# Weight tiles of 512 columns read with a column step of four, w_out four rows per descriptor, the band from 256-column products, and a new order of the first steps, in a fused convolution and SwiGLU kernel

## Chip, cores and metric

The kernel runs on one core of a Trainium2 chip. The metric is device time in microseconds (us) of one execution. Lower is better. Verdicts use a threshold of 2%. The differences in this case are far below it, near 0.1%, so most of the study is about which parts of a small change arrive in the time, and which do not.

## The reference

A causal convolution over the sequence (7 taps for each of 8 heads, the taps being a softmax of a small weight table), then a SwiGLU block. Shapes: x is 8 x 4096 x 192, so 32768 tokens of width 192; d_ff is 1536. All is float32 outside; the kernel computes in float16 with float32 accumulation.

```python
out  = einsum('hk,bskhg->bshg', softmax(weight), windows(x_pad))   # 7 taps, 8 heads
g    = out @ w_gate            # 192 -> 1536
val  = out @ w_val
y    = (g * sigmoid(g) * val) @ w_out                              # 1536 -> 192
```

## The kernel before

Tokens go through in 64 blocks of 512. A block has 12 *steps*; step n computes 128 of the 1536 hidden columns by three pairs of matmuls (gate on the upper 64 rows of the array, val on the lower 64, at once), a silu on ScalarE and a product on VectorE. *Slots* of down matmuls (times w_out) are put between the steps. The convolution of later blocks is a set of small matmuls with a band matrix, hidden among the steps.

The start is special. Nothing can run before the band is made from the 8 x 7 taps. The first four blocks' inputs (tiles xe) are convolved by `early(e)`, turned by matmuls in `eturn(e)`, and only then can gate steps run. All loads that cast from float32 to float16 are issued by GpSimd, in this order: input of block 0, first and second piece of the weights, input of block 1, third piece, w_out, more input.

```python
    def load_w(f0, f1):                       # gate and val columns f0 to f1, three DMAs
        for half, src, i0, i1, s0 in (...):
            nc.gpsimd.dma_start(out=w16[Q*half : Q*half+Q, i0:i1, f0:f1], in_=src[..., f0:f1]...)
    def load_wo(c0, c1):                      # 128 rows of w_out per chunk, 768 B each (f32)
        nc.gpsimd.dma_start(out=wo16[:, c0:c1, :], in_=moe_w_out[...].rearrange("(c p) d -> p c d", p=P))
    ...
    xe_load(0)
    load_w(0, 384)
    load_w(384, 1024)
    xe_load(1)
    load_w(1024, Dff)
    load_wo(0, 6)
    load_wo(6, NCH)
    # ... cut: more input loads, preparations of the band
    keep_warm(7)              # filler matmuls of 512 columns
    spread_taps()             # 16 tiny matmuls, then two spreads on VectorE
    keep_warm(2)
    make_wide()               # four products of 512 columns, copied out by ScalarE and VectorE
    early(0, ...)
    eturn(0, ...)
    # gate_val(n):
            nc.tensor.matmul(o, w16[p0 : p0 + Q, k, ts(j, P)], xc[b][k][p0 : p0 + Q, 0:TB], ...)
    # main loop, first block: early(1) after step 4, eturn(1) after step 6, slot 1 after step 7,
    # slot 2 (with early(2) inside) after step 10, eturn(2) after step 17;
    # a slot at step n waits for the silu of step n - 2 ("row halves swap banks")
```

## Time and profile before

| | before |
|---|---|
| median time | 793.78 us (792.71 to 794.28, 4 runs) |
| span of the profiled execution | 792.0 us |
| TensorE busy | 784.0 us |
| first gate matmul | 9.97 us |
| step 23 begins (all start effects are over) | 37.59 us |
| from step 36 to the end | 739.99 us |

The page's busy table and the chain of work that ended last (shares of the span, by engine):

```profile
PE 784.0 (99%) x12018; PEld 493.9 (62%) x12018; DVE 584.1 (74%) x933; ACT 522.2 (66%) x910; POOL 67.4 (9%) x93
...
PE 97%; DMA 1%; POOL 1%; DVE 0%; ACT 0%; issue 0%; POOLq 0%
```

TensorE is the limit nearly everywhere. Its costliest groups (line, engine, operation, output and inputs, partitions x elements, count; then busy us, mean ns of one, idle time before them):

```profile
L545 PE MATMUL val<-xc,w 64*128 64x512 f16 x2304 | 539.1, 376 | 0.2 <-DVE tm L486 0.2
L545 PE MATMUL gate<-xc,w 64*128 64x512 f16 x2304 | 539.2, 376 | 0.0
L545 PEld LDWEIGHTS <-w 64*128 64x128 f16 x4608 | 221.0, 94 | 212.7 <-issue 1.2
```

The matmuls of a pair overlap each other and the next pair: a duration of 376 ns does not mean that one takes 376 ns of TensorE. What counts is the spacing of the pairs, 0.215 us. The PEld line is the load of the weights into the array, 94 ns each, beside the matmuls.

The start on TensorE (timeline: start us, duration us, then as above, with idle time and what ended it in brackets):

```profile
5.43 1.58 PE L326 MATMUL taps<-spread,shift 128*128 128x512 f16 x4
7.57 0.83 PE L380 MATMUL cv<-xe,wide 64*64 64x72 f16 x64 [0.56 <-ACT wide L338]
8.89 1.14 PE L438 MATMUL turn<-ident,tme 128*128 128x128 f16 x15 [0.50 <-ACT tme L398]
9.97 0.39 PE L545 MATMUL gate<-xc,w 64*128 64x512 f16 x1
...
13.72 0.22 PE L380 MATMUL cv<-xe,wide 64*64 64x72 f16 x1
14.50 0.72 PE L380 MATMUL cv<-xe,wide 64*64 64x48 f16 x63 [0.56 <-DMA xe<-in_x_dram]
15.15 0.39 PE L545 MATMUL gate<-xc,w 64*128 64x512 f16 x1
...
30.45 0.72 PE L438 MATMUL turn<-ident,tme 128*128 128x128 f16 x10 [0.34 <-DVE o_sb L627]
```

early(0) waits for the band at 7.57 us; early(1) waits for the input of block 1, which lands at 14.46 us; and the second turn waits for the output copies of block 0 at 30.45 us.

### The profile page before, as it was taken

The page shows a single profiled execution, that of the slowest core. Times are in us where ns is not written, and L with a number is a line of the kernel's source. Part 1 is how long each engine was busy: PE and PEld are TensorE (multiplying, and loading weights), DVE is VectorE, ACT ScalarE, POOL GpSimd, SP SyncE. Part 2 cuts the span into 40 slices and gives each one's busy share as a digit, 9 for nine tenths or more (in the row PEclk, how much of TensorE's full clock was granted, in tenths as well). Part 3 has the DMA queues.
Part 4 walks back from the last instruction along what each step waited for, and adds up shares of the span by engine and source line. Part 5 has one row for each costly group of instructions (what it writes and reads, how often), then busy time and mean ns, then how long its engine had stood idle before and what let it go on. Part 6 is the DMA issues. An engine that isn't in the chain of part 4 may idle for free.

```text
span 792.0 us, 28590 instructions
## 1 busy us (share of the span) xinstructions
PE 784.0 (99%) x12018; PEld 493.9 (62%) x12018; DVE 584.1 (74%) x933; ACT 522.2 (66%) x910; POOL 67.4 (9%) x93
## 2 busy tenths in 40 slices
PE   8999999999999999999999999999999999999997
PEld 4666666666666666666666666666666666666665
DVE  7677777777777867767777777777777777777775
ACT  5676766666666666757666666666667667676664
POOL 8111010010100101001010000100001010000000
PEclk9999999999999999999999999999999999999999
DMA  9999577786857778567894769858587794726311
GB/s 131 149 204 146 125 116 118 164 124 146 105 120 152 129 147 119 120 126 125 155 140 113 117 112 165 128 133 118 112 154 121 150 115 118 136 81 116 80 42 42
DMA packets 214961, 99.23 MB, mean 125 GB/s; under 512 B 148776, under 2 KB 213936, under 8 KB 213936
## 3 DMA queue, kind: packets, MB, share of 16 engines
q1 hardware_dynamic: 167424, 78.75, 49.3%
q0 software_dynamic: 47136, 18.45, 21.7%
q8 instruction: 94, 1.54, 0.8%
q14 instruction: 35, 0.29, 0.1%
q10 hardware_dynamic: 272, 0.20, 0.1%
HBM read 36.90 MB, written 41.16 MB: 99 GB/s over the span
## 4 chain that ended last, share of the span: by engine, by line
PE 97%; DMA 1%; POOL 1%; DVE 0%; ACT 0%; issue 0%; POOLq 0%
PE gate L545 61%; PE acc L571 32%; PE cv L469 2%; PE val L545 1%; DMA xe<-in_x_dram 1%; POOL w L162 0%; POOL xe L97 0%; PE acc L592 0%; PE cv L380 0%; PE turn L438 0%; DVE h L556 0%; ACT sig L554 0%; DVE o_sb L627 0%; DVE tm L486 0%; ACT o_sb L731 0%
## 5 line engine op out<-in xcount | busy, mean ns | idle before, releaser
L556 DVE TENSOR_TENSOR h<-sig,val 128x512 f16<-128x512 f16 x768 | 507.7, 687 | 195.4 <-PE val L545 192.9
L554 ACT ACTIVATE sig<-gate 128x512 f16<-128x512 f32 x768 | 458.5, 597 | 234.9 <-PE val L545 207.4
L545 PE MATMUL val<-xc,w 64*128 64x512 f16 x2304 | 539.1, 376 | 0.2 <-DVE tm L486 0.2
L545 PE MATMUL gate<-xc,w 64*128 64x512 f16 x2304 | 539.2, 376 | 0.0
L545 PEld LDWEIGHTS <-w 64*128 64x128 f16 x4608 | 221.0, 94 | 212.7 <-issue 1.2
L571 PEld LDWEIGHTS <-h 64*128 64x128 f16 x6096 | 257.8, 94 | 66.0 <-issue 6.1
L571 PE MATMUL acc<-wo,h 64*128 64x192 f16 x6096 | 298.8, 243 | 0.0
L97 POOL DMA_DIRECT2D x<-in_x_dram x40 | 31.6, 792 | 437.0 <-ACT sig L554 429.9
L486 ACT CAST tm<-cv 128x480 f16<-128x480 f32 x60 | 30.6, 562 | 22.1 <-PE cv L469 22.1
L486 DVE CAST tm<-cv 128x480 f16<-128x480 f32 x60 | 36.6, 652 | 2.6
L627 DVE COPY o_sb<-acc 128x384 f32<-128x384 f32 x63 | 34.7, 550 | 0.0
L497 POOL COPY tm<-tm 128x1280 f16<-128x1280 f16 x15 | 18.8, 1252 | 137.3 <-DVE tm L486 129.1
L626 ACT COPY o_sb<-acc 128x384 f32<-128x384 f32 x63 | 30.1, 478 | 0.0
L469 PE MATMUL cv<-x,band 64*32 64x240 f16 x960 | 18.2, 265 | 0.0
L469 PEld LDWEIGHTS <-band 64*32 64x32 f16 x960 | 10.1, 91 | 4.9 <-issue 4.7
L132 POOL MEMSET x<- 6x192 f16 x7 | 1.7, 248 | 59.7 <-PE cv L469 59.6
L97 POOL DMA_DIRECT2D xe<-in_x_dram x9 | 6.0, 692 | 0.4 <-issue 0.3
L643 PE MATMUL warm<-fill 128*128 128x512 f16 x9 | 4.2, 628 | 1.2 <-DVE fill L91 1.2
L398 ACT CAST tme<-cv 128x288 f16<-128x288 f32 x8 | 2.9, 401 | 2.5 <-PE cv L380 2.5
L380 PE MATMUL cv<-xe,wide 64*64 64x48 f16 (+1 forms) x256 | 3.2, 192 | 1.1 <-ACT wide L338 0.6
L380 PEld LDWEIGHTS <-wide 64*64 64x64 f16 x256 | 2.7, 108 | 2.5 <-ACT wide L338 1.1
L438 PE MATMUL turn<-ident,tme 128*128 128x128 f16 x45 | 3.3, 220 | 0.8 <-ACT tme L398 0.5
(53 smaller groups left out, 40.0 us busy)
## 6 DMA issues: line engine op xcount, KB each, us to landing
out_dram<-o_sb SPq DMA_DIRECT2D x63, 384.0 KB
scr<-tm SPq DMA_DIRECT2D x105, 130.0 KB
x<-x SPq DMA_DIRECT2D x28, 480.0 KB
x<-in_x_dram POOLq DMA_DIRECT2D x24, 480.0 KB, 9.4
x<-in_x_dram POOLq DMA_DIRECT2D x7, 468.0 KB, 7.4
xc<-scr SPq DMA_TRANSPOSE x180
scr<-tm SPq DMA_DIRECT2D x15, 104.0 KB
wo<-in_moe_w_out_dram POOLq DMA_DIRECT2D x2, 288.0 KB, 6.3
```

Of the source, the lines that this page charges most:

```text
L97: nc.gpsimd.dma_start(out=t[p0 + i0 : p0 + i1, w0 - at : w1 - at, :], in_=bass.AP(tensor=x_flat.tensor, offset=(t0 + size * w0 - pad + i0) ...
L380: nc.tensor.matmul(o[Q * c : Q * c + Q, at : at + w], wide[Q * r : Q * r + Q, a, h, :], xe[e][Q * r : Q * r + Q, c : 2 * G : 2, h * grp : ...
L469: nc.tensor.matmul(banks[r][32 * c : 32 * c + 32, t * w : t * w + w], band[Q * r : Q * r + Q, h, :], x16[u][Q * r : Q * r + Q, NG * c : NG ...
L486: eng(tm[u][:, NG * r : NG * r + NG, 2 * grp * hp : 2 * grp * hp + 2 * grp].rearrange("p g (t e) -> p g t e", t=2), banks[r][:, 0 : 2 * w] ...
L497: seq(nc.gpsimd.tensor_copy(tm[u][:, :, SL * Q : 4 * Q], tm[u][:, :, 0:Q]))
L545: nc.tensor.matmul(o, w16[p0 : p0 + Q, k, ts(j, P)], xc[b][k][p0 : p0 + Q, 0:TB], start=(k == 0), stop=(k == SL - 1),)
L554: silu[n] = seq(nc.scalar.activation(sg, g, AF.Silu)).ins
L556: seq(nc.vector.tensor_tensor(hj, sg, v, op=ALU.mult))
L571: nc.tensor.matmul(acc[b][bank][:, s, :], hj[p0 : p0 + Q, ts(2 * bank + s, P)], wo16[p0 : p0 + Q, j, :], start=(not second and j == 0 and ...
L626: seq(nc.scalar.copy(o_sb[:, 0:2, :], acc[b][0]))
L627: seq(nc.vector.tensor_copy(o_sb[:, 2:4, :], acc[b][1]))
L643: nc.tensor.matmul(warm, fill[:, 0:P], fill, start=True, stop=True, skip_group_check=True,)
```

## The change

Its intent: make the band with less work; load equal pieces of 512 weight columns; load w_out in fewer, longer rows (four rows of w_out, 3072 B, are contiguous when hidden column 4p + e sits on partition p). The price of that is that the gate weights must be read with a column step of four. The first 22 steps get a new order. The diff, cut to its core:

```diff
-    w16 = wpool.tile([P, SL, Dff], fp16, tag="w16", name="w16")
+    WF = Dff // 3; E = WF // P                       # 512 columns, step 4
+    w16 = [wpool.tile([P, SL, WF], fp16, tag=f"w16{m}", name="w16") for m in range(3)]
@@ load_wo
-                out=wo16[:, c0:c1, :],
-                in_=moe_w_out[P * c0 : P * c1, :].rearrange("(c p) d -> p c d", p=P),
+                out=wo16[:, E * m : E * m + E, :].rearrange("p e d -> p (e d)"),
+                in_=moe_w_out[WF * m : WF * m + WF, :].rearrange("(p e) d -> p (e d)", p=P),
@@ the first input window: 56 rows, issued second; its tile cleared over 64 rows
-                windows(xe[e], 0, 0, EO, 0, 1, i0=pad)
                 windows(xe[e], 0, 0, EO, 1, w1)
+                windows(xe[e], 0, 0, EO, 0, 1, i0=pad, i1=Q - 2)
@@ loads
-    load_w(0, 384); load_w(384, 1024); xe_load(1); load_w(1024, Dff); load_wo(0, 6); load_wo(6, NCH)
+    load_w(0); load_w(1); xe_load(1); load_w(2); load_wo(0); load_wo(1); load_wo(2)
@@ band: 2 tap matmuls instead of 16, one spread of 256 columns instead of two of 512,
@@ four products of 256 columns instead of four of 512      [cut]
-    keep_warm(2)
+    keep_warm(5, P)                                  # fillers of 128 columns
@@ gate_val
-                        w16[p0 : p0 + Q, k, ts(j, P)],
+                        w16[m][p0 : p0 + Q, k, e::E],
@@ order of the first steps
-  early(1) after step 4, eturn(1) after 6, slots after 7, 10, 13, 16 (silu n - 2), eturn(2) after 17
+  early(1) after step 5, eturn(1) after 7, slots after 9, 11, 13 (silu n - 1), 16, eturn(2) after 18
```

More of the change, by code (lines that the diff above doesn't have):

```diff
@@ L150, in dup_x, with load_w @@
             )
-    w16 = wpool.tile([P, SL, Dff], fp16, tag="w16", name="w16")
+    WF = Dff // 3
+    E = WF // P
+    w16 = [
+        wpool.tile([P, SL, WF], fp16, tag=f"w16{m}", name="w16") for m in range(3)
+    ]
     wo16 = wpool.tile([P, NCH, D], fp16, tag="wo16", name="wo16")
-    def load_w(f0, f1):
+    def load_w(m):
+        f0, f1 = WF * m, WF * m + WF
         for half, src, i0, i1, s0 in (
@@ L162, in load_w @@
                 nc.gpsimd.dma_start(
-                    out=w16[Q * half : Q * half + Q, i0:i1, f0:f1],
+                    out=w16[m][Q * half : Q * half + Q, i0:i1, :],
                     in_=src[Q * s0 : Q * (s0 + i1 - i0), f0:f1].rearrange(
@@ L168, in load_w, with load_wo @@
             )
-    def load_wo(c0, c1):
+    def load_wo(m):
         seq(
             nc.gpsimd.dma_start(
-                out=wo16[:, c0:c1, :],
-                in_=moe_w_out[P * c0 : P * c1, :].rearrange("(c p) d -> p c d", p=P),
+                out=wo16[:, E * m : E * m + E, :].rearrange("p e d -> p (e d)"),
+                in_=moe_w_out[WF * m : WF * m + WF, :].rearrange(
+                    "(p e) d -> p (e d)", p=P
+                ),
             )
@@ L182 @@
     seq(nc.gpsimd.iota(pid, pattern=[[0, 1]], base=0, channel_multiplier=1))
-    jid = small("jid", [P, P], i32)
-    seq(nc.gpsimd.iota(jid, pattern=[[1, P]], base=0, channel_multiplier=0))
+    jn = small("jn", [P, 4, Q], i32)
+    seq(nc.gpsimd.iota(jn, pattern=[[-16, 4], [1, Q]], base=0, channel_multiplier=0))
     xe_tile(0)
-    seq(nc.vector.memset(xe[0][0:pad, 0, :], 0.0))
+    seq(nc.vector.memset(xe[0][0:Q, 0, :], 0.0))
     xe_load(0)
-    load_w(0, 384)
-    load_w(384, 1024)
+    cid = small("cid", [P, P], i32)
+    seq(nc.gpsimd.iota(cid, pattern=[[1, P]], base=0, channel_multiplier=0))
+    load_w(0)
+    load_w(1)
     xe_tile(1)
     xe_load(1)
-    load_w(1024, Dff)
-    load_wo(0, 6)
-    load_wo(6, NCH)
+    load_w(2)
+    for m in range(3):
+        load_wo(m)
     xe_tile(2)
@@ L202 @@
             load_x(1, r, low=low)
-    pm_i = small("pm_i", [P, 1], i32)
-    seq(nc.vector.tensor_single_scalar(pm_i, pid, 31, op=ALU.bitwise_and))
-    pm = small("pm", [P, 1])
-    seq(nc.vector.tensor_copy(pm, pm_i))
-    jf = small("jf", [P, P])
-    seq(nc.vector.tensor_copy(jf, jid))
-    p32 = small("p32", [P, 1])
-    seq(nc.vector.tensor_tensor(p32, pid, pm, op=ALU.subtract))
-    pd = small("pd", [P, 1])
-    eye = small("eye", [P, 32], fp16)
+    pq_i = small("pq_i", [P, 1], i32)
+    seq(nc.vector.tensor_single_scalar(pq_i, pid, 15, op=ALU.bitwise_and))
@@ L214 @@
+    pq = small("pq", [P, 1])
+    seq(nc.vector.tensor_copy(pq, pq_i))
+    pk = small("pk", [P, 1])
+    seq(nc.vector.tensor_tensor(pk, pid, pq, op=ALU.subtract))
+    eye = small("eye", [P, 16], fp16)
     seq(
         nc.vector.tensor_scalar(
-            eye, jf[:, 0:32], scalar1=pm, scalar2=None, op0=ALU.is_equal
+            eye, jn[:, 0, 0:16], scalar1=pq, scalar2=None, op0=ALU.is_equal
         )
     )
-    seq(
-        nc.vector.tensor_scalar(pd, p32, scalar1=1.0 / 32, scalar2=None, op0=ALU.mult)
-    )
@@ L222 @@
-    both = small("both", [P, 1])
-    seq(nc.vector.tensor_tensor(both, pm, pd, op=ALU.add))
-    eyes = small("eyes", [P, 32, 2, H], fp16)
-    seq(
-        nc.scalar.copy(
-            eyes.rearrange("p j a h -> p j (a h)"),
-            eye.unsqueeze(2).to_broadcast([P, 32, 2 * H]),
-        )
-    )
-    shift = small("shift", [P, 2, 2, 2, Q], fp16)
-    def make_shift(n, i):
-        seq(
-            nc.vector.tensor_scalar(
-                shift[:, n, i],
-                jf[:, 0:Q].unsqueeze(1).to_broadcast([P, 2, Q]),
-                scalar1=both, scalar2=32.0 * n + 4.0 * i,
-                op0=ALU.subtract, op1=ALU.is_equal,
-            )
-        )
@@ L243 @@
-    wexp = small("wexp", [H, K + 1])
-    seq(nc.vector.memset(wexp[:, K : K + 1], 1e-9))
-    split = small("split", [H, 2, K + 1], fp16)
-    seq(nc.vector.memset(split, 0.0))
-    make_shift(0, 0)
-    make_shift(1, 0)
+    eyes = small("eyes", [P, 16, 2 * H], fp16)
+    seq(nc.scalar.copy(eyes, eye.unsqueeze(2).to_broadcast([P, 16, 2 * H])))
+    both = small("both", [P, 1])
+    seq(
+        nc.vector.scalar_tensor_tensor(
+            both, pk, 1.0 / 16, pq, op0=ALU.mult, op1=ALU.add
+        )
+    )
@@ new lines, with make_shift @@
+    wexp = small("wexp", [H, K + 1])
+    seq(nc.vector.memset(wexp[:, K : K + 1], 1e-9))
+    split = small("split", [H, 2, K + 1, 16], fp16)
+    seq(nc.vector.memset(split[:, :, K, :], 0.0))
+    shift = small("shift", [P, 4, 2, Q], fp16)
+    def make_shift(n):
+        seq(
+            nc.vector.tensor_tensor(
+                shift[:, n : n + 2],
+                jn[:, n : n + 2].unsqueeze(2).to_broadcast([P, 2, 2, Q]),
+                both.unsqueeze(2).unsqueeze(3).to_broadcast([P, 2, 2, Q]),
+                op=ALU.is_equal,
+            )
+        )
@@ L250 @@
+    make_shift(0)
     wmax = small("wmax", [H, 1])
@@ L254 @@
     seq(nc.scalar.activation(warmed, fill[:, 0:1], AF.Silu))
-    make_shift(0, 1)
+    make_shift(2)
     wsum = small("wsum", [H, 1])
@@ L258 @@
     seq(nc.vector.reciprocal(wsum, wsum))
+    wide_exp = wexp[:, 0:K].unsqueeze(2).to_broadcast([H, K, 16])
     seq(
-        nc.vector.tensor_scalar(
-            split[:, 0, 0:K], wexp[:, 0:K], scalar1=wsum, scalar2=None, op0=ALU.mult
+        nc.vector.tensor_tensor(
+            split[:, 0, 0:K],
+            wide_exp,
+            wsum.unsqueeze(2).to_broadcast([H, K, 16]),
+            op=ALU.mult,
         )
@@ L266 @@
             split[:, 1, 0:K],
-            wexp[:, 0:K],
+            wide_exp,
             wsum,
@@ L273 @@
     )
-    make_shift(1, 1)
-    tap = small("tap", [P, 2, 2, H], fp16)
-    spread = small("spread", [P, 2, 32, 2, H], fp16)
+    tap = small("tap", [P, 2 * H], fp16)
+    spread = small("spread", [P, 16, 2, H], fp16)
     def spread_taps():
         bank = apool.tile([P, TB], fp32, tag="acc0", name="tapbank")
-        for i in range(2):
-            for a in range(2):
-                c0 = (2 * i + a) * H
-                for d in range(4):
-                    k = 4 * i + d
-                    seq(
-                        nc.tensor.matmul(
-                            bank[32 * d : 32 * d + 32, c0 : c0 + H],
-                            split[:, a, k : k + 1].to_broadcast([H, 32]),
-                            eye[0:H, 0:H],
-                            start=(c0 == 0),
-                            stop=True,
-                            skip_group_check=True,
-                            tile_position=(0, 32 * d),
-                        )
-                    )
-        seq(
-            nc.vector.tensor_copy(
-                tap.rearrange("p i a h -> p (i a h)"), bank[:, 0 : 4 * H]
-            )
-        )
-        for i in range(2):
-            seq(
-                nc.vector.tensor_tensor(
-                    spread[:, i].rearrange("p j a h -> p j (a h)"),
-                    eyes.rearrange("p j a h -> p j (a h)"),
-                    tap[:, i]
-                    .rearrange("p a h -> p (a h)")
-                    .unsqueeze(1)
-                    .to_broadcast([P, 32, 2 * H]),
-                    op=ALU.mult,
-                )
-            )
+        for a in range(2):
+            seq(
+                nc.tensor.matmul(
+                    bank[:, a * H : a * H + H],
+                    split[:, a].rearrange("h k q -> h (k q)"),
+                    eye[0:H, 0:H],
+                    start=(a == 0),
+                    stop=True,
+                    skip_group_check=True,
+                )
+            )
+        seq(nc.vector.tensor_copy(tap, bank[:, 0 : 2 * H]))
+        seq(
+            nc.vector.tensor_tensor(
+                spread.rearrange("p j a h -> p j (a h)"),
+                eyes,
+                tap.unsqueeze(1).to_broadcast([P, 16, 2 * H]),
+                op=ALU.mult,
+            )
+        )
     wide = small("wide", [P, 2, H, Q], fp16)
@@ L322, in make_wide @@
         ]
-        for i in range(2):
-            for n in range(2):
-                seq(
-                    nc.tensor.matmul(
-                        banks[n],
-                        shift[:, n, i].rearrange("p r i -> p (r i)"),
-                        spread[:, i].rearrange("p j a h -> p (j a h)"),
-                        start=(i == 0),
-                        stop=(i == 1),
-                    )
+        for n in range(4):
+            c0 = 16 * 2 * H * (n % 2)
+            seq(
+                nc.tensor.matmul(
+                    banks[n // 2][:, c0 : c0 + 16 * 2 * H],
+                    shift[:, n].rearrange("p r i -> p (r i)"),
+                    spread.rearrange("p j a h -> p (j a h)"),
+                    start=(n % 2 == 0),
+                    stop=True,
+                    skip_group_check=True,
                 )
+            )
         seq(nc.vector.tensor_copy(pf, pid))
@@ L346, in make_wide @@
             nc.vector.tensor_scalar(
-                ident, jf, scalar1=pf, scalar2=None, op0=ALU.is_equal
+                ident, cid, scalar1=pf, scalar2=None, op0=ALU.is_equal
             )
@@ L540, in gate_val @@
         v = ppool.tile([P, TB], fp32, tag="val", name="val")
+        m, e = divmod(j, E)
         for k in range(SL):
@@ L638, with keep_warm @@
     warm = ppool.tile([P, TB], fp32, tag="gate", name="warm")
-    def keep_warm(count):
+    def keep_warm(count, width=TB):
         for _ in range(count):
@@ L643, in keep_warm @@
                 nc.tensor.matmul(
-                    warm, fill[:, 0:P], fill, start=True, stop=True,
-                    skip_group_check=True,
+                    warm[:, 0:width], fill[:, 0:P], fill[:, 0:width],
+                    start=True, stop=True, skip_group_check=True,
                 )
@@ L663, with work @@
         work = None
-        if n == 4:
-            def work():
-                early(1, (*acc_banks, gate_bank))
-        elif n in (10, 19):
-            def work(e=2 if n == 10 else 3):
+        if n in (11, 19):
+            def work(e=2 if n == 11 else 3):
                 early(e, (gate_bank, gate_bank, val_bank))
@@ L679 @@
         gate_val(n)
-        if j % 3 == 1:
-            after = silu[n - 2] if n >= 2 else None
-            if j == 1:
-                if b:
-                    slot(3, b - 1, after)
-            elif j == 4:
-                if b:
-                    slot(4, b - 1, after)
-                if work:
-                    work()
-            else:
-                slot(1 if j == 7 else 2, b, after, work)
-        if u == 0:
-            if ls == 6:
-                eturn(1, (*acc_banks, gate_bank))
-            if ls == 17:
-                eturn(2, (*acc_banks, gate_bank))
-            if ls == 20:
-                eout(3)
-            if ls == 21:
-                efetch(3)
+        if n == 5:
+            early(1, (*acc_banks, gate_bank))
+        elif n == 7:
+            eturn(1, (*acc_banks, gate_bank))
+        elif n in (9, 11):
+            slot(1 if n == 9 else 2, b, silu[n - 1], work)
+        elif n == 13:
+            slot(3, 0, silu[n - 1])
+        elif j % 3 == 1 and b:
+            k = {1: 3, 4: 4, 7: 1, 10: 2}[j]
+            slot(k, b - 1 if j < 7 else b, silu[n - 2], work if j > 4 else None)
+            if j == 4 and work:
+                work()
+        if n == 18:
+            eturn(2, (*acc_banks, gate_bank))
+        elif n == 20:
+            eout(3)
+        elif n == 21:
+            efetch(3)
         if u + 1 < NU:
```

## The prediction

> **What bounds the kernel now.** TensorE. The busy table gives it 784.0 of 792.0 us, and the chain that ended last lies 97% on it (gate 61%, down product 32%). By the timeline a gate/val pair of 64-row matmuls takes 0.215 us (eight pairs from 34.17 to 35.89 us) and 24 down matmuls 0.99 us: 2304 x 0.215 + 6096/24 x 0.99 + 16 us of convolution is about 763 us of matmul work, which the change leaves. It can win only in the first 10 us (first gate at 9.97 us) and in small PE gaps up to about 45 us.
>
> **What it removes and moves, with times of before.**
> 1. Band. 16 tap matmuls (0.36 us) become 2; two 0.38 us spreads become one of half the columns; four 512-column products (1.58 us) become four of 256. With fewer VectorE preparations I expect the early convolution, now at 7.57 us, 0.6-0.8 us sooner.
> 2. The first weight tile has 512 columns instead of 384. By the issue list its three loads land at about 7.9, 8.5 and 9.4 us; with a third more bytes on full DMA engines (busy share 1.03 in 5-10 us) and a longer iota before them, the last lands around 10.1. This eats most of point 1: the first gate starts near 9.3-9.8, and its last pair waits.
> 3. The limit is the second block's input. Its load lands about 14.5 us and early(1) waits there (0.7 us in the wait list). Bytes ahead of it are unchanged. The new order puts one more step (0.644 us) before that wait, so 0.4-0.5 us is kept.
> 4. w_out goes from 1536 rows of 768 B (f32) to 384 of 3072 B: less descriptor work while DMA is over-full (15-30 us), but no PE wait names w_out: about 0.
> 5. The second turn moves one step later; it now waits 0.34 us on the output copy (29.9-30.45 us): +0.3 us.
> 6. The down slots at steps 9, 11, 13 wait for the silu of the step just before. A silu takes 0.60 us, a gate step 0.644: up to 0.2 us of wait each, -0.3 us together.
>
> Sum, with a little from the band: 0.9 us won, 792.6 us, under 0.2%. Nothing touches the end.
>
> **The one large risk: the column step.** Weight columns are read eight bytes apart, 4608 times. Now a load takes 94 ns beside 0.215 us pairs, with no gap on PE. The Trainium skill, "TensorE: Matmul & The Clock Gate", section on weight-path perf modes, has fast weight load "packed or strided", steps up to 1,024 elements; "SBUF — State Buffer", Door 1, wants two hits per 16-byte line for full rate, which a step of four f16 just gives. No load in this trace has such a step. Even loads twice as long should hide behind the pair. I expect 94 ns and 0.215 us unchanged. If the pair grew by 5%, the kernel would lose about 25 us.
>
> **What would show it.** Timeline: taps products half as long; early convolution at 6.7-7.0 us; early(1) still waiting for its input, to 14.3-14.8 us, then step 6 following instead of step 5. Groups: gate weight loads at 94 ns. From 60 to 780 us: same length.
>
> **What would make it wrong.** A strided weight load that is slower or disturbs the moving reads; the second block's input landing at another time; larger silu waits; a cold clock after the longer wait.
>
> Predicted 792.6 us, 8 in 10 within 791.0 to 794.2; faster by over 2%: 0.01, within 2%: 0.92, slower: 0.07.

## The result, and the profile after

The kernel after takes 792.86 us in the median (792.09 to 795.08, 4 runs) against 793.78 us of before. The ratio is 0.9995 with a 95% interval of 0.9972 to 1.0018. A ratio here is the mean time of one kernel's fast runs over that of the other's of the same rounds, so it is not quite the ratio of the medians. The predicted 792.6 lies 0.3 us from the median. The timed runs alone do not even settle the sign; the traces show, for one execution of each kernel, where each tenth of a microsecond went.

The same lines of the page after:

```profile
PE 783.5 (99%) x12007; PEld 526.7 (67%) x12007; DVE 582.9 (74%) x928; ACT 522.1 (66%) x910; POOL 67.6 (9%) x95
...
L538 PE MATMUL val<-xc,w 64*128 64x512 f16 x2304 | 539.2, 376 | 0.2 <-DVE tm L478 0.2
L538 PE MATMUL gate<-xc,w 64*128 64x512 f16 x2304 | 539.3, 376 | 0.0
L538 PEld LDWEIGHTS <-w 64*128 64x128 f16 x4608 | 254.0, 110 | 183.9 <-issue 1.6
```

The strided weight loads take 110 ns instead of 94, which adds 33 us of load time (254.0 - 221.0). No matmul pays for it: the busy time of TensorE and the mean of a matmul are unchanged. And the timeline of the start:

```profile
5.11 1.01 PE L317 MATMUL taps<-spread,shift 128*128 128x256 f16 x4
6.68 0.82 PE L372 MATMUL cv<-xe,wide 64*64 64x72 f16 x64 [0.56 <-ACT wide L330]
8.01 1.04 PE L430 MATMUL turn<-ident,tme 128*128 128x128 f16 x15 [0.50 <-ACT tme L390]
9.01 0.38 PE L538 MATMUL gate<-xc,w 64*128 64x512 f16 x1
...
13.48 1.03 PE L372 MATMUL cv<-xe,wide 64*64 64x72 f16 x64
13.79 0.61 PEld L372 LDWEIGHTS <-wide 64*64 64x64 f16 x63 [0.21 <-DMA xe<-in_x_dram]
14.44 0.40 PE L538 MATMUL gate<-xc,w 64*128 64x512 f16 x1
...
29.41 1.01 PE L430 MATMUL turn<-ident,tme 128*128 128x128 f16 x15
```

From the early convolution to the first gate everything comes 0.9 to 1.0 us sooner. early(1) still waits for its input, now on the side of the weight loads (the PEld line). At 14.44 us it is now step 6 that follows early(1), where before it was step 5 at 15.15 us. The second turn no longer waits. Step 23 begins at 36.40 us instead of 37.59. From step 36 to the end it takes 740.00 us, before 739.99. The load of that input, from the chain of work that ended last (start, duration), before and then after:

```profile
7.55 6.91 DMA xe<-in_x_dram
7.74 6.01 DMA xe<-in_x_dram
```

So the profiled gain of 1.2 us lies wholly in the start:

| stretch | before | after | won |
|---|---|---|---|
| input of block 1 has landed | 14.46 | 13.74 | 0.72 |
| first step after early(1) begins | 15.15 (step 5) | 14.44 (step 6) | 0.71, and one step (0.645) more is done |
| from there to step 23 | 22.44 for 18 steps | 21.96 for 17 steps | 0.48, less the step: -0.17 |
| step 23 begins | 37.59 | 36.40 | 0.71 + 0.645 - 0.17 = 1.19 |

The reasons to be tested: (S) equal rows of 512 columns move faster through DMA, so the input of block 1 lands sooner; its rival (X), the 56-row first load relieves one late DMA engine. (O) The new order is worth half of the gain by itself. (B) The band's gain of 0.9 us at the first gate is mostly hidden behind that input load. (L) The slower weight loads are hidden; the rival is that they cost a little everywhere. And an open question: why one of the four timed runs of after took 795.08 us, some 2.5 us more than the other three.

### The profile page after: what moved, and what is told of

Its sections match the earlier page's. It is cut to its first block, busy times and chain, and to the rows that moved or that the text cites. A ratio compares the mean times of both kernels' runs of the same rounds, so it can differ in the third digit from the quotient of the medians.

```text
span 790.9 us, 28567 instructions
## 1 busy us (share of the span) xinstructions
PE 783.5 (99%) x12007; PEld 526.7 (67%) x12007; DVE 582.9 (74%) x928; ACT 522.1 (66%) x910; POOL 67.6 (9%) x95
## 4 chain that ended last, share of the span: by engine, by line
PE 97%; POOL 1%; DMA 1%; DVE 0%; ACT 0%; issue 0%; POOLq 0%
PE gate L538 61%; PE acc L564 32%; PE cv L461 2%; PE val L538 1%; DMA xe<-in_x_dram 1%; POOL w L167 0%; POOL xe L97 0%; PE acc L585 0%; PE cv L372 0%; PE turn L430 0%; DVE h L549 0%; ACT sig L547 0%; DVE tm L478 0%; ACT o_sb L718 0%; DVE o_sb L620 0%
## 5 line engine op out<-in xcount | busy, mean ns | idle before, releaser
L538 PEld LDWEIGHTS <-w 64*128 64x128 f16 x4608 | 254.0, 110 | 183.9 <-issue 1.6
L461 PEld LDWEIGHTS <-band 64*32 64x32 f16 x960 | 10.1, 91 | 4.9 <-issue 4.7
L636 PE MATMUL warm<-fill 128*128 128x512 f16 (+1 forms) x12 | 3.9, 496 | 1.2 <-DVE fill L91 1.2
L372 PE MATMUL cv<-xe,wide 64*64 64x72 f16 (+1 forms) x256 | 3.2, 192 | 0.7 <-ACT wide L330 0.6
```

Source lines behind the costliest of these rows:

```text
L372: nc.tensor.matmul(o[Q * c : Q * c + Q, at : at + w], wide[Q * r : Q * r + Q, a, h, :], xe[e][Q * r : Q * r + Q, c : 2 * G : 2, h * grp : ...
L461: nc.tensor.matmul(banks[r][32 * c : 32 * c + 32, t * w : t * w + w], band[Q * r : Q * r + Q, h, :], x16[u][Q * r : Q * r + Q, NG * c : NG ...
L538: nc.tensor.matmul(o, w16[m][p0 : p0 + Q, k, e::E], xc[b][k][p0 : p0 + Q, 0:TB], start=(k == 0), stop=(k == SL - 1),)
L636: nc.tensor.matmul(warm[:, 0:width], fill[:, 0:P], fill[:, 0:width], start=True, stop=True, skip_group_check=True,)
```

## Experiments

Twelve kernels ran, and all gave correct results. A name with a_ is the kernel after with one part changed (a_best with two, a_again with none), one with b_ the kernel before with one part changed. This table sums up what the traces show, one profiled execution each (us, except the DMA column, which is the GB/s moved from 6 to 12 us, by the windows view; "clock full" is when the trace's record of the granted clock goes from half to full; the fifth column is the step right after early(1)):

| kernel | clock full | GB/s | input 1 landed | step after early(1) | first gate | step 23 | span |
|---|---|---|---|---|---|---|---|
| before | 6.54 | 143 | 14.46 | 15.15 | 9.97 | 37.59 | 792.0 |
| b_order | 6.63 | 142 | 14.13 | 15.06 | 9.97 | 36.99 | 791.5 |
| b_xe56 | 3.90 | 150 | 14.05 | 14.75 | 9.08 | 37.19 | 791.7 |
| b_sizes | 5.86 | 163 | 13.81 | 14.51 | 9.55 | 36.95 | 791.5 |
| after | 6.21 | 167 | 13.74 | 14.44 | 9.01 | 36.40 | 790.9 |
| a_again | 4.44 | 182 | 13.43 | 14.12 | 8.59 | 36.08 | 790.5 |
| a_xe58 | 10.42 | 168 | 13.90 | 15.15 | 10.06 | 37.11 | 791.6 |
| a_contig | 6.48 | 179 | 13.02 | 14.13 | 9.00 | 36.06 | 790.7 |
| a_slots | 4.65 | 184 | 13.60 | 14.30 | 8.59 | 36.03 | 790.5 |
| a_oldband | 5.24 | 184 | 13.20 | 14.40 | 9.32 | 36.36 | 791.0 |
| a_warm | 3.97 | 162 | 14.18 | 14.88 | 8.45 | 36.84 | 791.3 |
| a_best | 3.84 | 171 | 14.49 | 15.19 | 8.95 | 36.92 | 791.5 |
| a_fewwarm | 13.05 | 178 | 13.74 | 16.17 | 9.52 | 39.43 | 794.0 |
| a_step12 | 6.11 | 174 | 12.58 | 21.64 | 13.66 | 43.66 | 798.1 |

From step 36 to the end it took 739.99 to 740.21 us in all fourteen. The rest of the program may be taken as a constant to about 0.2 us. The start itself differs between executions: step 23 began at 36.40 and 36.08 us in two executions of the same kernel (after and a_again), so a difference of a few tenths between two single traces can be chance.

### 1. The loads alone: b_sizes

```diff
-    load_w(0, 384)
-    load_w(384, 1024)
+    load_w(0, 512)
+    load_w(512, 1024)
```

> The kernel before, with the weights loaded in three loads of 512 columns in place of 384, 640 and 512; nothing else changes, and the tile and the column step stay as before. Theory S (equal 512-column rows move faster: packets of 1024 B flowed at about 175 KB/us after, those of 768 and 1280 B at about 120 to 146 KB/us before): the second block's input lands near 13.7 us instead of 14.46 and the span falls by about 0.7 us, to about 791.3. Theory X (the 58-row first load leaves one DMA engine late, and every later load waits for that engine): it still lands at 14.3 to 14.6 us, and the span stays at about 792.0.

Measured: input 1 landed at 13.81 us, step 23 began at 36.95 (0.64 sooner), span 791.5, one time of 793.23 against 793.74 (the four kernels of sections 1 to 3 have one run each, of unknown state, so that only their traces count). S fits. The windows view shows it as a rate. Before (window, length, busy us and instruction counts of each engine, granted clock, mean DMA share, GB/s):

```profile
6.00:12.00 6.00, 4.94 (x101) 2.70 (x99) 3.04 (x8) 3.00 (x7) 4.37 (x8) 1.00 1.08 143
```

and b_sizes:

```profile
6.00:12.00 6.00, 4.89 (x104) 2.79 (x102) 3.42 (x9) 3.30 (x8) 5.20 (x9) 1.00 1.17 163
```

All three traces with pieces of 384, 640 and 512 columns moved 142 to 150 GB/s in this stretch; all eleven with equal pieces 162 to 184. The landings of input 1 are less clear: 14.05 to 14.46 us in the three (mean 14.2), 12.58 to 14.49 in the eleven (mean 13.6). So the rates stand apart, but the 0.65 to 0.72 us of these pairs of traces are in part scatter, and before's own landing is the latest of its three.

Why equal pieces move faster stays open. The packets do not say that short rows are dear: in the first 16 us the median packet of 768, 1024 and 1280 B took 79, 98 and 116 ns in every trace that has such packets, and since both ways have 768 rows for the first 1024 columns, 384 x 79 + 384 x 116 = 74.9 us of engine time and 768 x 98 = 75.3 us are the same. What differs is the sum with all slow packets in it: the packets of those 1024 columns took 93.4 us in before, 88.0 in b_order and 87.3 in b_xe56, and 80.5 to 89.3 in the eleven with equal pieces (89.3 in after). The means differ by 5.4 us, over 16 engines 0.3 us. What made some packets slow, no run shows.

### 2. The first input load: b_xe56 and a_xe58

```diff
-                windows(xe[e], 0, 0, EO, 0, 1, i0=pad)
                 windows(xe[e], 0, 0, EO, 1, w1)
+                windows(xe[e], 0, 0, EO, 0, 1, i0=pad, i1=Q - 2)
@@ and the memset of its tile over 64 rows; a_xe58 is the reverse, on the kernel after
```

> The kernel before, with only the first input load changed: 56 rows instead of 58, issued after the big one, its tile cleared over 64 rows. Theory X: the weights' last packets no longer straggle, the third load of the first weight piece lands near 8.5 us instead of 9.40 and the second block's input near 13.7 instead of 14.46; span about 791.3. Theory S: no landing moves by over 0.2 us, span about 792.0.

Measured: input 1 landed at 14.05 and the first piece's last load at 9.18 us; span 791.7, time 793.48. Neither theory's numbers came. b_order, whose loads are those of before, landed input 1 at 14.13 and that first piece at 8.70, so landings with the same loads scatter by 0.3 to 0.7 us from one execution to the next, and the 14.05 here is no sign of X.

> The kernel after, with only that first input load put back (58 rows, issued first). Theory X: the first weight tile's last load lands near 9.6 us instead of 8.77 and the second block's input near 14.5 instead of 13.74; span about 791.6 instead of 790.9. Theory S: landings within 0.2 us of after, span about 790.9.

Measured: input 1 landed at 13.90, within 0.2 us of after, as S has it; the first piece's last load landed at 9.43, near X's number. Whether 58 rows delay the first piece by some tenths is left open. It does not matter here, since input 1 is what is waited for. But this execution brought something else, the late clock. The granted clock went full only at 10.42 us, and the chain to the first gate ran at half speed:

```profile
5.11 1.01 PE L317 MATMUL taps<-spread,shift 128*128 128x256 f16 x4
6.68 1.17 PE L372 MATMUL cv<-xe,wide 64*64 64x72 f16 x64 [0.56 <-ACT wide L330]
8.35 1.78 PE L430 MATMUL turn<-ident,tme 128*128 128x128 f16 x15 [0.49 <-ACT tme L390]
10.06 0.55 PE L538 MATMUL gate<-xc,w 64*128 64x512 f16 x1
```

The early convolution begins at 6.68 us exactly as in after, then takes 1.17 us instead of 0.82 and the turn 1.78 instead of 1.04. The first gate comes 1.05 us later. Step 23 comes 0.71 later. The span of 791.6 is thus a matter of the clock and not of the 58 rows.

### 3. The order alone: b_order

```diff
-  early(1) after step 4, eturn(1) after 6, slots after 7, 10, 13 (silu n - 2), eturn(2) after 17
+  early(1) after step 5, eturn(1) after 7, slots after 9, 11, 13 (silu n - 1), eturn(2) after 18
```

> The kernel before, with only the new order of the first 22 gate steps (early(1) after step 5, slots at 9, 11 and 13 waiting for the silu of the step before, second turn after step 18). My theory: early(1) still ends its wait at 14.5 us but one more step lies before it (0.644 us won), the three slots lose about 0.2 us each, the second turn wins 0.5 us: step 23 starts 0.5 to 0.6 us sooner than before (37.59 us), so at about 37.0, span about 791.4. A rival, that the order is worth nothing by itself and the gain comes from the loads alone: step 23 at 37.4 to 37.8.

Measured: step 23 at 36.99, 0.60 us sooner; span 791.5; time 793.34. O holds. Luck of the load had little part in it: had input 1 landed at 14.46 as in before, the step after early(1) would have begun 0.09 us later (14.46 + 0.69), which leaves 0.51.

The 0.60 of the order and the 0.64 of b_sizes come near to the 1.19 of the whole change, but they do not simply add. In b_order TensorE, with the old band, reached early(1) at 14.39, after its input had landed (14.13), and waited for nothing:

```profile
14.39 0.73 PE L380 MATMUL cv<-xe,wide 64*64 64x72 f16 x64
```

A sooner load alone would have won nothing more there. TensorE had to come sooner as well, and in after it does (13.48): that is the new band's share.

In eight of the traces the step after early(1) begins 0.69 or 0.70 us after input 1 has landed (0.65 us is the early convolution itself). In the other six TensorE arrived after the load. So two chains race to this point: the load, and the band with five or six steps behind it.

### 4. The band: a_oldband

The band of before (16 tap matmuls, two spreads, four 512-column products, two 512-column fillers) is put back into the kernel after.

```diff
-    keep_warm(5, P)
+    keep_warm(2)
@@ and the preparations, spread_taps and make_wide as before
```

> The kernel after with the band of before put back (16 tap matmuls, two spreads, four 512-column products, two wide fillers); the loads, the column step and the order of steps stay. Theory 1 (the new band's gain lies behind the second block's input load): first gate at 9.5 to 10.0 us in place of 8.6 to 9.0, but step 23 at 36.1 to 36.6 as in after (36.40 and 36.08), best runs within 0.2 us of after's. Rival: the gain arrives, step 23 at 36.8 or later. Theory 2 (the runs at 795 of the kernel after, 3 of 10, come from a clock released late because the new band keeps TensorE less busy in the first 7 us): no run over 794 here. Rival: as many as after.

Measured: median 792.85 us (792.81 to 793.57), ratio to before 0.9989 (0.9976 to 1.0001). First gate at 9.32, sooner than I had expected, later than 9.01 and 8.59 with the new band. Step 23 at 36.36, against 36.40 and 36.08 in two executions of after. By these three traces 0.3 to 0.7 us at the first gate became 0.0 to 0.3 us at step 23. But their loads and clocks differ. Here input 1 had landed at 13.20, sooner than in both, and TensorE was the later of the two chains:

```profile
13.73 0.73 PE L387 MATMUL cv<-xe,wide 64*64 64x72 f16 x64
```

Step 6 began at 14.40, where this load would have allowed 13.90 (13.20 + 0.70): with it, 0.5 us of the band's gain would have arrived. And with the clock as late as in b_order (full at 6.63, here at 5.24) the old band gets to step 6 at 15.06, 0.6 us after the 14.44 of after. So, as an estimate from these traces, the band brings 0.0 to 0.6 us, more the later the clock and the sooner the load; B holds in part. The times agree: I had expected the best runs within 0.2 us of after's, and they are 0.8 us above (792.81, 791.98); the median is 0.3 us above that of a_warm (section 8), which has the new band and ran in the same rounds. No run was over 794, as theory 2 has it.

### 5. The column step: a_contig and a_step12

a_contig reads side by side again and loads w_out as before, row by row:

```diff
-                        w16[m][p0 : p0 + Q, k, e::E],
+                        w16[m][p0 : p0 + Q, k, ts(e, P)],
-                in_=... .rearrange("(p e) d -> p (e d)", p=P)
+                in_=... .rearrange("(e p) d -> p e d", p=P)
```

> The kernel after with the column step alone undone: weight columns read side by side, and w_out loaded as 768 B rows again, still in three loads. My theory (a longer load hides behind the matmul pair): weight loads of the gate line take 94 ns instead of 110, their spacing stays 0.215 us, step 36 to the end stays 740.0 plus or minus 0.2, and the time is within 0.1% of after. The w_out loads and the later input loads land up to 1 us later, with no TensorE wait for them. Rival (the strided load costs TensorE time): step 36 to the end is shorter by 1 us or more.

a_step12 goes the other way: one tile of 1536 columns, step twelve (24 bytes), and one load of w_out with twelve rows per descriptor.

```diff
-    WF = Dff // 3
+    WF = Dff                                        # E becomes 12
-    for m in range(3):
-        load_wo(m)
+    load_wo(0)
@@ the weights still come in three loads of 512 columns, into the one tile
```

> The kernel after with one weight tile of 1536 columns read with a step of twelve (24 bytes), and w_out in one load of twelve rows per descriptor. Theory: a load takes longer than 110 ns, since no two of its reads now share a 16-byte line (the Trainium skill, SBUF - State Buffer, Door 1), I guess 130 to 200 ns, but still hides behind the pair, so step 36 to the end stays at 740 to 742. Rival: two loads no longer fit beside a pair and the spacing grows beyond 0.215 us, step 36 to the end over 745. Either way the first step now needs all three weight loads, which land near 15.3 us, so the start is about 5 us later and the total 797 to 799 in the first case.

The loads from the gate tile in a_contig (count, then least, median and largest ns):

```profile
L538 PEld LDWEIGHTS <-w x4608: 92/94/96, 9.0 to 783.2; 64*128 64x128 f16 x192
```

and in a_step12:

```profile
L537 PEld LDWEIGHTS <-w x4608: 134/138/165, 13.7 to 790.7; 64*128 64x128 f16 x192
```

Steps of one, four and twelve columns make 94, 110 and 138 ns. From step 36 to the end: 740.16, 740.00 and 740.00 us. L holds: even the 138 ns load hides beside the pair. a_contig took 792.60 us (792.47 to 793.01), ratio 0.9986 (0.9974 to 0.9998); a_again, in the same rounds, 792.34. So the step of four costs nothing, and w_out in longer rows gains nothing that arrives: its three loads landed at 15.79, 16.88 and 17.93 us row by row, at 16.02, 16.95 and 18.06 in a_again. I had expected them up to 1 us later. Nothing waited for them in either.

a_step12 took 799.77 us, ratio 1.0076, a bit above what I had expected, and the reason is the clock again. TensorE waited 4.62 us for the third weight load, the clock fell to half from 12.94 to 19.77 us, and pairs came 0.43 us apart:

```profile
13.66 0.64 PE L537 MATMUL gate<-xc,w 64*128 64x512 f16 x1 [4.62 <-DMA w<-in_moe_w_gate_dram]
14.28 0.64 PE L537 MATMUL val<-xc,w 64*128 64x512 f16 x1
14.29 0.64 PE L537 MATMUL gate<-xc,w 64*128 64x512 f16 x1
14.72 0.63 PE L537 MATMUL val<-xc,w 64*128 64x512 f16 x1
```

### 6. The kernel after once more: a_again

> The kernel after once more, unchanged, to learn how much its start differs between executions and to narrow the interval. My theory: steady state is the same (from gate step 36 to the end 740.0 us, as in all six traces so far), the spread sits in the first 15 us, above all in when the granted clock goes to full (3.90 to 10.42 us so far). Step 23 starts at 36.4 to 37.1, ratio to before 0.9985 to 0.9995. Rival, that the 0.9 us of the first result was chance: ratio at 1.000.

Measured: median 792.34 us (791.98 to 795.42, 6 runs); before 793.60 (11 runs); ratio 0.9992 (0.9977 to 1.0006). Four of its runs lie at 792.0 to 792.4, two at 794.85 and 795.42. Step 23 began at 36.08, even sooner than my range. With the first result, the kernel after has ten runs: seven from 791.98 to 793.08, three from 794.85 to 795.42. Before has 34 runs over all rounds, from 792.71 to 794.85, median 793.7, mean 793.8. The median of after is 792.5, the mean 793.2. So a usual execution wins about 1.2 us, and some executions give it back.

### 7. The slots: a_slots

```diff
-        elif n in (9, 11):
-            slot(1 if n == 9 else 2, b, silu[n - 1], work)
+        elif n in (8, 11):
+            slot(1 if n == 8 else 2, b, silu[n - 2], work)
```

> The kernel after with the first two down slots at steps 8 and 11 instead of 9 and 11, each waiting for the silu two steps back instead of one. Theory: the 0.2 us holes ahead of the down matmuls at 18.1 and 20.6 us go, so from step 6 to step 23 it takes 21.5 to 21.7 us instead of 21.96, and the total falls by 0.3 us. Rival: at step 8 the slot meets the copies of the turned tile that still hold its banks, or w_out's first load, and gives the gain back: 21.9 to 22.1.

Measured: from step 6 to step 23 it took 21.73 us instead of 21.96, so 0.23 us, less than I had expected. The list of who waited for whom (15 to 30 us, the weight loads of the down matmuls: total us, times, longest) shows what went. After:

```profile
PEld L564 <- ACT sig L547: 1.5, 3, 0.5
```

a_slots:

```profile
PEld L564 <- ACT sig L547: 0.5, 1, 0.5
```

Before has no such wait there. The matmuls hide most of each wait. A step with the slot after it, from its start to the next step's, took 1.85, 3.11 and 1.85 us in after (steps 9, 11 and 13), against 1.79, 2.96 and 1.64 in before (7, 10 and 13): 0.42 us lost together. In a_slots the first two took 1.79 and 2.96 as in before, so 0.06 and 0.15 were won back. The slot at step 19, which no one had in view, also takes longer since the change, 2.62 us against 2.41 in before: it now comes one step after the second turn, where before it came two steps after. b_order shows the same 2.62; the profile names no cause. The time was 793.13 us in the median (792.27 to 794.97, 5 runs), ratio 1.0000 (0.9988 to 1.0013): two of the five runs were again at 794.65 and 794.97, and the gain drowns in them.

### 8. The slow runs: a_warm, a_fewwarm, a_best

By the Trainium skill, "TensorE: Matmul & The Clock Gate", Part 1, TensorE starts at half clock and goes full when it was busy enough over a free-running window of 3.4 us. The traces agree: the stretch at full clock was 785.07 us in ten of them, which is 230 windows of 3.413 us, and it began anywhere from 3.84 to 6.63 us, in two kernels at 10.42 and 13.05. The new band has less filler work, so I suspected that more executions now miss a window. a_warm adds fillers, a_fewwarm takes nearly all away.

```diff
@@ a_warm
     make_wide()
+    keep_warm(5, P)
     early(0, ...)
+    warm = ppool.tile([P, TB], fp32, tag="val", name="warm")
+    keep_warm(5, P)
     eturn(0, ...)
@@ a_fewwarm
-    keep_warm(7)
+    keep_warm(2)
-    keep_warm(5, P)
```

> The kernel after with ten more filler matmuls of 128 columns, five ahead of the early convolution and five ahead of the first turn, where TensorE waits for copies. Theory 2: no run over 794, median 792.3 or less, the clock full by 7.1 us at the latest in the profile. Rival (the runs at 795 have another cause): about 3 of 10 runs near 795 as in after. If the fillers themselves delay the chain, first gate later than 9.1 us.

> The kernel after with only two filler matmuls of 512 columns at the start and none of the five of 128: the suspected cause of the slow runs, made on purpose. Theory 2: the granted clock goes full only at 7 us or later in every execution, the first gate comes at 9.5 to 10.5, and the time is 793.5 to 796, which the runs at 795 match. Rival: it stays within 0.5 us of after's usual 792.3, because the second block's input load hides the loss; then a late clock cannot explain the runs at 795.

a_warm: median 792.53 us (792.02 to 793.09, 5 runs), ratio 0.9984 (0.9971 to 0.9996), no run over 794; the median I had expected at 792.3 or less. a_oldband had none either. a_fewwarm: 794.14 us (794.04 to 795.83, 4 runs), ratio 1.0003. Its profiled execution went to full clock at 13.05 us, its first gate pairs came 0.41 to 0.43 us apart, and the step after early(1) began at 16.17 us, 1.73 later than in after, though input 1 landed at 13.74 in both. So a late clock can cost that much. Its three other runs, 794.04 to 794.21, are 1.5 to 1.7 us above the median of a_warm. They have no trace: that their clock was as late is likely and not shown.

But this does not settle the runs at 795. The profiled run of a_fewwarm is the one of 795.83, and over 1 us of it comes from something else, near 25 us, at full clock:

```profile
23.65 0.71 PE L372 MATMUL cv<-xe,wide 64*64 64x72 f16 x63
25.50 0.18 PE L372 MATMUL cv<-xe,wide 64*64 64x48 f16 x1 [1.14 <-issue]
```

The last of 64 matmuls is held although its weights are loaded and the profile shows nothing that it waits for ("issue", 1.14 us; it began 1.33 us after the matmul before it). In the trace's instruction queue the second 16 KB packet after the start began at 23.02 us; in the twelve traces other than this one and a_step12 it began at 17.1 to 19.8. A late instruction fetch fits, but it was seen once, and no run took it away. I did not catch one of after's own slow runs in a profile. Of the 21 executions with the new band and its few fillers (after, a_again, a_slots, a_contig, a_xe58) 5 are over 794.5; of the 15 with more fillers (a_oldband, a_warm, a_best) none. That points to the clock, and does not prove it. Before, with the old band, has 3 of 34 there (794.62 to 794.85). And two numbers speak against the clock alone: a_xe58, full only at 10.42 us, took 793.36, and the three usual runs of a_fewwarm stay 0.4 us or more below those five. The mean clock listed with each run does not help: it reads 1.0 for a_xe58 too.

a_best joins the two mends, fillers and slots:

> The kernel after with both mends: the ten fillers of a_warm and the slots at steps 8 and 11 of a_slots. If both hold, from step 6 to step 23 it takes 21.7 us (21.96 in after, 21.73 in a_slots), no run is over 794, and the median is 792.0 to 792.4, below before's by 1.2 us or more. If the runs at 795 come from something other than the clock, for example from the instruction fetch that held one matmul of a_fewwarm for 1.33 us, one or two of the runs are again over 794.

Measured: median 792.17 us (791.97 to 793.34, 5 runs); before 793.54 in the same rounds; ratio 0.9982 (0.9968 to 0.9996). From step 6 to step 23 it took 21.73 us, as expected, and no run was over 794. The profiled run is its slowest, 793.34: input 1 landed only at 14.49 us. It has the lowest median of all kernels here, but it ran on another chip (8) than the other eleven experiments (0), with its own runs of before. Against before the interval excludes 1; against after, whose usual runs are as fast, the lead is 0.2 to 0.3 us of median, across chips, and not proved.

## Why the prediction was right, point by point

The time was right, and its main reading, that TensorE's steady work is untouched and only the first 45 us can win, was exact: 740.00 us from step 36 on against 739.99. Several of its points were not.

1. *Band, early convolution "0.6-0.8 us sooner".* It came 0.89 us sooner (6.68 against 7.57). Right, slightly under-sized, and part is luck of the clock: with the old band it began at 6.76 to 7.61 in five executions, with the new one at 6.05 to 6.68 in eight (a_fewwarm aside).
2. *"The last lands around 10.1. This eats most of point 1: the first gate starts near 9.3-9.8."* Wrong. The last load of the first tile landed at 8.77 us and the first gate began at 9.01. The step that failed is scaling the landing by bytes at a fixed rate: with a third more bytes the first piece landed at 8.62 to 9.43 us in the eleven traces with equal pieces, against 8.70 to 9.40 in the three with the old ones. The rate from 6 to 12 us was 167 GB/s instead of 143, and 163 in b_sizes, which changed nothing else; why is open (section 1).
3. *"The limit is the second block's input … lands about 14.5 us … 0.4-0.5 us is kept."* The mechanism was right: eight traces show the step after early(1) 0.69 to 0.70 us after that landing. The landing was mis-sized, 13.74 instead of 14.3 to 14.8, in part for the reason of point 2 and in part by luck (12.58 to 14.49 in the traces with equal pieces). So the full step of 0.645 us was kept, and 0.71 us of earlier landing came on top. That 0.71 arrived only because TensorE was there in time (13.48); with the old band and a clock like before's it would have come at 14.39 (b_order).
4. *w_out, "about 0".* Right; a_contig undid it and lost nothing.
5. *Second turn "+0.3 us".* Right in kind; from the start of step 17 (before) or 18 (after) to the next step it went from 2.19 to 1.69 us, so +0.5. But the slot at step 19, now one step after the turn and not two, lost 0.21 us, which the prediction lacked; the net is near its +0.3 by luck.
6. *Slots "-0.3 us together".* Right in kind, slightly under-sized: 0.06 + 0.15 + 0.21 = 0.42 us. a_slots won the first two back.
7. *"I expect 94 ns and 0.215 us unchanged."* The first half was wrong, 110 ns. The half that carried the time was right. Its reason, that even loads twice as long should hide, was tested up to 47% longer (a_step12).

The sum was better than its parts. The points as I had costed them (0.45 + 0.3 - 0.3) make 0.45 us; the rest of the 0.9 I had put down to the band without a figure. Measured in the two traces, point 3 brought 1.36 us instead of 0.45 (0.71 of it needed both the sooner load and the sooner band), the turn brought 0.5, and the slots took 0.42 and 0.21. That the sum came out at 0.9 is thus partly luck. So the usual run wins about 1.2 us, 0.3 more than predicted, and the occasional run at 795 takes half of it back in the mean (0.6 us won by the means of 10 and 34 runs). The prediction named "a cold clock after the longer wait" as a risk, but not that it would be a matter of luck from one execution to the next.

## What to carry to other kernels

Where two chains race to one point, here a load and a string of matmuls, a gain in the chain that arrives first is worth nothing until the other moves: find which one arrives last, and by how much, before rewriting the other. Weight loads have slack as long as they hide beside the matmuls, so a layout that makes them 17% or even 47% longer may be free; read the spacing of the matmuls, not the duration of the load. For differences of 0.1%, cut the trace into stretches rather than time the whole kernel: the stretch from step 6 to step 23 took 21.96 us in five traces, where whole runs scatter by 2 us and the first step after the load by 1 us. And gains of two changes that feed such a race cannot be added up from runs with one change each. And filler matmuls that look like waste can bring the clock to full sooner (without most of them it was full only at 13.05 us in a_fewwarm): count them before trimming.

## What the Trainium skill lacked or had wrong

- "TensorE: Matmul & The Clock Gate", section on LDWEIGHTS, has a time by columns alone. It lacks the column step: a 128-column f16 load took 94, 110 and 138 ns with steps of 1, 4 and 12 elements. Its section on weight-path perf modes allows steps up to 1,024 elements but says no cost.
- "SBUF — State Buffer", Door 1, has full rate as long as two reads share a 16-byte line. A step of four f16 gives exactly two per line, and the load was already 16 ns longer than with a step of one. Where they differ, the measurement decides. That the line is what costs the time is not shown.
- "DMA: Bandwidth & Descriptors" lacks the cost by row length of loads that cast from f32 to f16: the median packet of 768, 1024 and 1280 B (f16) took 79, 98 and 116 ns, the mean one 93 to 103, 98 to 111 and 131 to 141, and the 6 to 12 us stretch moved 142 to 150 GB/s with mixed pieces and 162 to 184 with equal ones.
- "TensorE: Matmul & The Clock Gate", Part 1, says that the window is free-running and that the ramp is under 1% of a typical span. Both agree here (full clock from 3.84 to 13.05 us; a_fewwarm, the latest, lost under 2 us by it, about 0.2% of the span). It lacks how busy a window must be: a_xe58 missed one that, by the spacing of 3.413 us, ended near 7.0 us, where after, with the same TensorE work, passed one that ended at 6.21. The busy time that the profile shows is not the measure: a_best passed a window with 2.63 us of busy TensorE in it, a_xe58 missed that one with 2.85.
- No page that I read gives the size of a stall from a late instruction fetch; one matmul here was held for 1.14 us by what looks like one.
